# Column-tiled attention work gathered into bursts of four head groups, with a third dense PSUM bank

## Chip, cores, metric

One core of one Trainium2 chip. The metric is the time of one execution on the device in microseconds (us), median of several runs.

## The reference, cut to what matters

```python
def _A_ref(x, wq, wk, wv, wo, beta):      # S=2048, D=1024, H=32 heads of Dh=32, N=4 segments of L=512
    ...
    for s in range(N):
        logits = jnp.einsum('bhqd,bhkd->bhqk', qs, ks) * scale + mask     # causal within the segment
        a_dot = jnp.einsum('bhqk,bhkd->bhqd', _softmax(logits), vs)
        pq = phi(qs)
        num = jnp.einsum('bhld,bhde->bhle', pq, M)                        # memory of earlier segments
        den = jnp.einsum('bhld,bhd->bhl', pq, z)[..., None] + 1e-06
        outs.append(g * num / den + (1.0 - g) * a_dot)
        pk = phi(ks)
        M = M + jnp.einsum('bhld,bhle->bhde', pk, vs)
        z = z + jnp.einsum('bhld->bhd', pk)
    ...
h  = x + _A_ref(_layernorm(x), A_wq, A_wk, A_wv, A_wo, A_beta)
h2 = h + _B_ref(_layernorm(h), B_w1, B_w3, B_w2)      # (silu(h w1) * (h w3)) w2, F=3584
```

## The kernel before

The kernel first writes down all operations as a graph, then a list scheduler with a cost model of its own fixes the order of each engine, once, as the program is built. A table named SHIFT moves the priorities of single steps; it was tuned by search. Each engine is given its list in that order, with semaphores where it needs the work of another.

TensorE (PE below) works in three modes: full 128x128 matmuls (projections, output projection, feed-forward, memory), scores tiled in four blocks of 32 rows (one 32-wide head each), and probabilities times values, tiled in four blocks of 32 columns. A *mode run* is an unbroken sequence of matmuls in one mode; a *seam* is the change from one mode to the next. Four heads make a head group; there are eight in each of four segments. Scores of one operation fill PSUM banks 0 to 3, ScalarE takes their exponential in one instruction, GpSimd masks the diagonal blocks. Then one column-tiled run computes the numerator (bank 4) and the denominator (bank 5) of one head group. In the code `et` holds the exponentials, `pq` is phi of the queries, and `Mb` (or `Mbf`) and `zsel` hold the memory M and z:

```python
    def dense_group(self, late=False):                  # all full-mode work rotates through two banks
        g = Group([(6,), (7,)],
                  ("att", [(4,), (5,), (0,), (1,), (2,), (3,)]) if late else None, True)
    ...
    def pair(self, s, pr):                              # two head groups a, b: five score operations
        ta = self.scores(s, [(a, 0, 0)])
        tb = self.scores(s, [(a, 3, 384), (a, 1, 0)])
        tc = self.scores(s, [(a, 2, 0), (b, 2, 256)])
        self.finish(s, a, ...)                          # column run of a
        ta = self.scores(s, [(b, 0, 0)])
        tb = self.scores(s, [(b, 3, 384), (b, 1, 0)])
        self.finish(s, b, ...)                          # column run of b
    ...
    def finish(self, s, g, pq, pieces):
        gn, gd = self.queue(4), self.queue(5)
        ...                                             # memory read: Mb x pq to bank 4, zsel x pq to bank 5
        def emit(e, gr):
            for what, kc in order:                      # 2 x 4 key chunks x 4 heads = 32 matmuls
                b = (gn if what == "n" else gd).banks[0]
                for j in range(4):
                    r = slice(32 * j, 32 * j + 32)
                    lhsT = v[:, kc, g, r] if what == "n" else self.ones32[:, :]
                    ins.append(e.matmul(self.ps[r, b * 512 + 128 * kc:(b + 1) * 512], lhsT,
                                        pieces[kc][:, j, :], ..., tile_position=(0, 32 * j)))
        ...
        # then, per head group, on VectorE: transpose of bank 5, reciprocal, spread back by
        # transposes, and numerator x reciprocal read straight from bank 4
```

In the scheduler's model a change of mode costs PE 105 ns (`SWITCH = 105.0`).

The softmax here doesn't subtract the row's maximum and nothing guards it: scores larger than these inputs give would overflow.

Of the kernel before, what the change touches and what calls it, by code (L numbers as in the profile page):

```python
# [8 lines left out]
ALU = mybir.AluOpType  # L9
# [9 lines left out]
    0: (-342, 0), 1: (-212, 0), 2: (315, 0), 3: (-6, 1), 4: (101, 1), 5: (384, 0), 6: (-38, -1),  # L19
    7: (122, 0), 8: (556, 0), 9: (281, 0), 10: (-218, 0), 11: (-173, 1), 12: (92, 0),  # L20
    13: (-735, 1), 14: (323, 0), 15: (210, -1), 16: (-189, 0), 17: (-979, 0), 18: (265, 0),
    19: (414, 1), 20: (812, 0), 21: (7, 0), 22: (-103, -1), 23: (-657, 1), 24: (40, -1),
    25: (51, 0), 26: (-292, 0), 27: (612, 0), 28: (-340, 0), 29: (-227, 0), 30: (188, 0),
    31: (-321, -1), 32: (-2, 0), 33: (4, 0), 34: (388, 0), 35: (368, 1), 36: (-278, -1),
    37: (-458, -1), 38: (-508, 0), 39: (-303, 0), 40: (-61, 0), 41: (-280, 0), 42: (-55, 0),
    43: (-21, 0), 44: (-7, 0), 45: (4, 0), 46: (-6, -1), 47: (24, 0), 48: (38, 0), 49: (21, 0),
    50: (22, 0), 51: (134, 0), 52: (-162, -1), 53: (-133, 0), 54: (644, 0), 55: (76, -1),
    56: (-700, 1), 57: (80, 1), 58: (10, 0), 59: (-308, 0), 60: (-682, 1), 61: (-29, 0),
    62: (637, 0), 63: (-187, -1), 64: (-20, 0), 65: (11, 0), 66: (-3, 0), 67: (-210, -1),
    68: (-668, -1), 69: (2, 0), 70: (-662, 0), 71: (4, 0), 72: (11, 0), 73: (85, 0), 74: (8, 0),  # L30
    75: (9, 0), 76: (-10, 0), 77: (-18, 0), 78: (-424, 1), 79: (-9, 0), 81: (4, 0), 82: (-3, 0),
    83: (656, 0), 84: (-370, 0), 85: (2, 0), 86: (-540, 0), 87: (-294, 0), 88: (-87, 0),
    89: (-186, 0), 90: (-4, 0), 91: (39, 0), 92: (47, 0), 93: (-178, 1), 94: (68, 0),
    95: (-77, -1), 96: (138, 0), 97: (-1331, 0), 98: (-563, 1), 99: (-902, 0), 100: (421, -1),
    101: (446, 0), 102: (956, 1), 103: (87, 0), 104: (-505, -1), 105: (229, -1), 106: (573, -1),
    107: (325, 0), 108: (61, 0), 109: (312, -1), 110: (-29, -1), 111: (-643, -1), 112: (509, 1),
    113: (1416, 1), 114: (-608, -1), 115: (29, 0), 116: (283, 0), 117: (11, 0), 118: (-372, 1),
    119: (158, 1), 120: (-538, 0), 121: (-447, 0), 122: (42, 0), 123: (-489, 1), 124: (980, 0),
    125: (-266, 1), 126: (46, 1), 127: (-514, 1), 128: (-469, 1), 129: (-522, -1),
    130: (-229, 0), 131: (-210, 1), 132: (-1177, 1), 133: (270, 1), 134: (158, 0), 135: (-8, 0),  # L40
    136: (-47, 1), 137: (-1057, 0), 138: (29, 0), 139: (-110, 0), 140: (-355, -1),
    141: (-284, 0), 142: (-49, 0), 143: (-109, 0), 144: (-709, 1), 145: (40, 1), 146: (-104, 0),
    147: (-4, 0), 148: (-579, 0), 149: (-21, 0), 150: (43, 0), 151: (281, -1), 152: (131, 1),
    153: (-257, -1), 154: (-13, 0), 155: (-55, 0), 156: (20, 0), 157: (52, 0), 158: (224, -1),
    159: (-30, 0), 160: (240, -1), 161: (161, 0), 162: (-21, 0), 163: (-245, -1),
    164: (-118, 1), 165: (-21, 0), 166: (-32, 0), 167: (-330, 1), 168: (-643, -1),
    169: (373, -1), 170: (79, -1), 171: (790, -1), 172: (1, 0), 173: (117, 0), 174: (-3, 0),
    175: (-82, -1), 176: (19, -1), 177: (-1009, -1), 178: (116, 0), 179: (41, 0), 180: (63, -1),
    181: (-4, 0), 182: (-84, -1), 183: (-321, -1), 184: (-374, 0), 185: (332, 0),
    186: (-385, 0), 187: (410, 0), 188: (47, 0), 189: (83, -1), 190: (847, 0), 191: (-320, -1),  # L50
    192: (328, 0), 193: (-577, -1), 194: (-101, 0), 195: (-1451, 1), 196: (-91, 0),
    197: (583, -1), 198: (90, 0), 199: (-229, 1), 200: (-723, 1), 201: (-152, 1),
    202: (-627, 1), 203: (48, 0), 204: (280, 0), 205: (41, 0), 206: (344, 1), 207: (-444, 0),
    208: (-567, -1), 209: (-278, -1), 210: (54, 0), 211: (153, 0), 212: (-267, 0),
    213: (380, 1), 214: (-438, 1), 215: (649, 1), 216: (851, 0), 217: (954, -1), 218: (-218, 0),
    219: (130, 1), 220: (348, 0), 221: (-71, -1), 222: (-788, 0), 223: (-750, 0), 224: (-94, 0),
    225: (220, 1), 226: (6, -1), 227: (-279, 1), 228: (-660, -1), 229: (96, -1), 230: (213, 1),
    231: (270, 0), 232: (-172, 0), 233: (-91, 0), 234: (-773, 0), 235: (103, -1),
    236: (-161, 0), 237: (89, 0), 238: (-205, -1), 239: (486, -1), 240: (-177, 0),
    241: (-150, 0), 242: (-352, 0), 243: (-260, 0), 244: (44, -1), 245: (-107, 0),  # L60
    246: (174, -1), 247: (44, 0), 248: (19, 0), 249: (-252, 0), 250: (-441, 0), 251: (-26, 0),
    252: (41, 0), 253: (11, 0), 254: (30, 0), 255: (688, -1), 256: (764, 0), 257: (-364, 1),
    258: (-52, 0), 259: (17, 0), 260: (124, -1), 261: (18, 0), 262: (-206, 0), 263: (47, 0),
    264: (-179, 0), 265: (244, 0), 266: (-625, -1), 267: (93, 0), 268: (345, 0), 269: (-62, 1),
    270: (132, 0), 271: (836, 1), 272: (-541, 0), 273: (-49, -1), 274: (49, -1), 275: (-89, 1),
    276: (64, 0), 277: (-306, 1), 278: (-125, 0), 279: (-41, -1), 280: (-760, 0), 281: (213, 0),
    282: (264, -1), 283: (252, 1), 284: (-39, 0), 285: (-388, 0), 286: (-156, 1),
    287: (-713, -1), 288: (-309, -1), 289: (-975, 1), 290: (-695, 0), 291: (73, 0),
    292: (158, 0), 293: (174, 0), 294: (721, 0), 295: (166, 0), 296: (61, -1), 297: (-412, 1),
    298: (-61, -1), 299: (403, 0), 300: (59, 0), 301: (-53, 0), 302: (-52, 0), 303: (31, 0),  # L70
    304: (-297, -1), 305: (744, -1), 306: (201, -1), 307: (24, 0), 308: (-166, 0), 309: (74, 1),
    310: (327, 0), 311: (-160, 0), 312: (181, 0), 313: (-750, -1), 314: (-245, 0),
    315: (-612, 0), 316: (300, 0), 317: (-492, 0), 318: (39, 0), 319: (-48, 0), 320: (554, 0),
    321: (1, 0), 322: (-118, 0), 323: (304, -1), 324: (-636, -1), 325: (-454, -1),
    326: (-727, 0), 327: (-79, 1), 328: (-195, 1), 329: (-254, 1), 330: (678, 0),
    331: (-332, -1), 332: (164, 1), 333: (-102, 0), 334: (535, 0), 335: (-105, -1),
    336: (-708, 0), 337: (71, 0), 338: (124, 0), 339: (-288, 0), 340: (-155, 1),
    341: (-179, -1), 342: (9, 0), 343: (-423, -1), 344: (-103, 0), 345: (-407, 0), 346: (27, 1),
    347: (17, -1), 348: (-96, 0), 349: (-655, -1), 350: (-229, 1), 351: (-289, -1),
    352: (-65, 0), 353: (-196, 1), 354: (-41, 1), 355: (21, -1), 356: (582, 0), 357: (-490, 1),  # L80
    358: (843, 0), 359: (520, 0), 360: (-823, 0), 361: (-30, -1), 362: (202, 0), 363: (-203, 1),
    364: (-305, 0), 365: (-433, 0), 366: (-311, 0), 367: (-161, 0), 368: (-53, 0),
    369: (-59, 0), 370: (635, 0), 371: (12, 0), 372: (9, 0), 373: (15, 0), 374: (233, 0),
    375: (-416, -1), 376: (179, 0), 377: (-757, -1), 378: (-331, 0), 379: (-42, -1),
    380: (21, 0), 381: (-340, -1), 382: (-768, 0), 383: (102, -1), 384: (224, 0),
    385: (-181, 1), 386: (148, 0), 387: (426, 0), 388: (249, 1), 389: (133, -1), 390: (346, 0),
    391: (-513, -1), 392: (211, 0), 393: (-434, -1), 394: (134, 0), 395: (100, 0),
    396: (147, -1), 397: (-333, -1), 398: (277, -1), 399: (-32, 0), 400: (-287, 0),
    401: (-117, 0), 402: (-11, 0), 403: (92, -1), 404: (-88, 0), 405: (-239, -1), 406: (148, 0),
    407: (-639, -1), 408: (65, 1), 409: (14, -1), 410: (393, -1), 411: (-251, 0), 412: (316, 0),  # L90
    413: (-180, -1), 414: (252, 1), 415: (-47, 0), 416: (182, 0), 417: (-336, 0),
    418: (-321, 0), 419: (-879, 0), 420: (-332, -1), 421: (252, 0), 422: (-453, 1),
    423: (-5, 0), 424: (28, -1), 425: (-319, -1), 426: (-202, 0), 427: (-22, 0), 428: (333, 0),
    429: (-129, -1), 430: (139, 1), 431: (-66, -1), 432: (-200, 1), 433: (-770, 1),
# [64 lines left out]
class Graph:  # L159
# [150 lines left out]
    def schedule(self):  # L310
# [33 lines left out]
        def can_start(o):  # L344
            g = o.group
            if isinstance(g, Both):
                todo = [x for x in g.parts if x.banks is None]
                for x in todo:
                    if x.after is not None and x.after.banks is None:
                        return False  # L350
# [919 lines left out]
```

## Time and profile before

| | before |
|---|---|
| median | 910.39 us (909.82 to 911.53; the 3 runs known when the prediction was made) |
| span of the profiled run | 908.6 us |
| PE busy | 900.9 us, 99% |
| VectorE, ScalarE, GpSimd busy | 432.4, 293.0, 174.7 us |
| mode runs of PE | 95 full, 80 row-tiled, 32 column-tiled |

The prediction shows the lines of this profile on which it rests. One more piece of PE's timeline shows what a wait looks like there, as against the short extra time at a change of mode (columns: start, length, engine, line, output<-inputs, shape, count; in brackets the idle time before and what ended it):

```profile
36.08 1.02 PE L697 MATMUL ps<-xnT,wp 128*128 128x512 bf16 x4 [0.43 <-ACT kT L720]
37.76 0.40 PE L994 MATMUL ps<-qT,kT 32*128 32x128 bf16 x8 [0.66 <-ACT et L1007]
```

These are 0.43 and 0.66 us in which PE stood still for ScalarE. A change of mode leaves no bracket: it shows only as a distance between two starts that is longer than the columns need.

*Excess* is the time from one run of a mode to the next, less its columns at 2.4 columns per ns (in tiled runs four tiles stream at once, so a quarter of that), less 2.5 ns for each full matmul. It holds both mode changes and waits; a wait ahead of a run falls to the run before it.

### The profile page before, as it was taken

The numbers are of one execution on the slowest core, as the hardware profiler recorded it, in microseconds if no ns is written. First come the engines' busy times: TensorE is split into PE (matmuls) and PEld (weight loads), VectorE is DVE, ScalarE is ACT, GpSimd is POOL, SyncE is SP. The second block draws the span as 40 slices with busy tenths as digits, with TensorE's granted clock in tenths as the row PEclk, the third lists the DMA queues.
The fourth block names the chain that finished last, engine by engine and source line by source line (L and its number), as shares of the span: only waits on it lengthen the run. The fifth ranks groups of instructions, "written<-read, shape, count | busy, mean of one in ns | idle before, by whom it ended". The sixth has DMA issues, their size and how long they took to land.

```text
span 908.6 us, 13100 instructions
## 1 busy us (share of the span) xinstructions
PE 900.9 (99%) x5564; PEld 406.9 (45%) x5564; DVE 432.4 (48%) x742; ACT 293.0 (32%) x311; POOL 174.7 (19%) x273
## 2 busy tenths in 40 slices
PE   8999999999999999999999999999999999999998
PEld 5444444444444344444444444444444444444445
DVE  3777878768776764554442332211343334431111
ACT  5877776677766711111111110000121111110000
POOL 3544645565564410000000000000000000000000
PEclk9999999999999999999999999999999999999999
DMA  9976663824264164827161222012123212301110
GB/s 297 248 186 186 140 174 94 210 66 119 84 163 116 48 217 131 201 77 174 54 167 47 70 70 69 24 47 78 51 86 93 70 50 67 93 24 40 35 41 30
DMA packets 146425, 96.27 MB, mean 106 GB/s; under 512 B 45376, under 2 KB 133568, under 8 KB 146368
## 3 DMA queue, kind: packets, MB, share of 16 engines
q1 hardware_dynamic: 146368, 95.45, 38.3%
q8 instruction: 44, 0.72, 0.3%
q14 instruction: 13, 0.11, 0.0%
HBM read 76.55 MB, written 8.39 MB: 93 GB/s over the span
## 4 chain that ended last, share of the span: by engine, by line
PE 97%; DMA 1%; ACT 1%; DVE 0%; issue 0%; SPq 0%
PE ps L697 90%; PE ps L1064 4%; PE ps L994 3%; DMA wp<-in_A_wq_dram 1%; ACT et L1007 1%; DMA xs<-in_A_x_dram 0%; ACT xnT L720 0%; PE ps L709 0%; SPq L294 0%; ACT kT L720 0%; DVE xs L826 0%; DVE ob L1180 0%; DVE lnst L817 0%
## 5 line engine op out<-in xcount | busy, mean ns | idle before, releaser
L697 PE MATMUL ps<-hnT,w1b 128*128 128x512 bf16 x896 | 219.5, 379 | 0.0
L697 PE MATMUL ps<-hnT,w3b 128*128 128x512 bf16 x896 | 219.0, 379 | 0.4 <-DVE t L1151 0.3
L1148 ACT ACTIVATE sg<-ps 128x512 bf16<-128x512 f32 x112 | 66.9, 597 | 430.4 <-PE ps L697 430.3
L697 PE MATMUL ps<-w2b,hm 128*128 128x512 bf16 (+1 forms) x924 | 199.0, 373 | 0.0
L1151 DVE SCALAR_TENSOR_TENSOR t<-sg,ps 128x512 bf16<-128x512 bf16 x112 | 76.9, 687 | 209.5 <-ACT sg L1148 209.3
L1007 ACT ACTIVATE et<-ps 128x2048 bf16<-128x2048 f32 x80 | 149.9, 1874 | 40.5 <-PE ps L1064 22.5
L697 PEld LDWEIGHTS ps<-w2b,hm 128*128 128x128 bf16 x924 | 90.4, 98 | 103.3
L697 PEld LDWEIGHTS ps<-hnT,w3b 128*128 128x128 bf16 x896 | 87.0, 98 | 107.0 <-issue 2.3
L697 PEld LDWEIGHTS ps<-hnT,w1b 128*128 128x128 bf16 x896 | 87.4, 98 | 105.6 <-issue 7.9
L1012 POOL TENSOR_SCALAR_AFFINE_SELECT et<-et 128x512 bf16<-128x512 bf16 x128 | 88.6, 709 | 121.9 <-ACT et L1007 121.7
L1156 DVE SCALAR_TENSOR_TENSOR hm<-t,ps 128x512 bf16<-128x512 bf16 x112 | 76.8, 686 | 43.4 <-PE ps L697 40.8
L1180 DVE TENSOR_TENSOR ob<-hr,ps 128x512 bf16<-128x512 bf16 (+1 forms) x33 | 22.1, 671 | 125.0 <-PE ps L697 125.0
L697 PE MATMUL ps<-xnT,wp 128*128 128x512 bf16 (+1 forms) x352 | 62.0, 321 | 1.9 <-ACT xnT L720 1.5
L697 PE MATMUL ps<-hnT,wp 128*128 128x512 bf16 x256 | 62.5, 380 | 0.3 <-DMA wp<-in_A_wq_dram 0.3
L697 PE MATMUL ps<-wo,oT 128*128 128x512 bf16 x256 | 62.5, 379 | 0.0
L697 PEld LDWEIGHTS ps<-xnT,wp 128*128 128x128 bf16 x352 | 27.7, 98 | 28.7 <-issue 4.2
L1075 DVE STREAM_TRANSPOSE T<-ps 128x512 f32<-128x512 f32 x32 | 22.9, 716 | 31.4 <-PE ps L1064 31.3
L697 PEld LDWEIGHTS ps<-wo,oT 128*128 128x128 bf16 x256 | 24.1, 98 | 29.7 <-issue 2.1
L697 PEld LDWEIGHTS ps<-hnT,wp 128*128 128x128 bf16 x256 | 23.3, 98 | 30.3 <-issue 3.8
L1101 POOL TENSOR_TENSOR Nm<-Nm,R1b 128x512 f32<-128x512 f32 x23 | 29.2, 1271 | 23.6 <-DVE R1b L1090 23.6
L994 PE MATMUL ps<-qT,kT 32*128 32x128 bf16 (+3 forms) x512 | 31.7, 301 | 0.8 <-ACT et L1007 0.8
L823 POOL TENSOR_SCALAR lnve<-lnmv 128x1 f32<-128x1 f32 x31 | 8.3, 268 | 125.0 <-DVE lnmv L819 125.0
(84 smaller groups left out, 614.2 us busy)
## 6 DMA issues: line engine op xcount, KB each, us to landing
w1b<-in_B_w_dram SPq DMA_DIRECT2D x28, 512.0 KB, 3.9
w3b<-in_B_w_dram SPq DMA_DIRECT2D x28, 512.0 KB, 3.8
wp<-in_A_wv_dram SPq DMA_DIRECT2D x8, 1024.0 KB, 6.8
wp<-in_A_wq_dram SPq DMA_DIRECT2D x7, 1024.0 KB, 5.6
wp<-in_A_wk_dram SPq DMA_DIRECT2D x7, 1024.0 KB, 6.4
w2b<-in_B_w_dram SPq DMA_DIRECT2D x7, 1024.0 KB, 8.0
xs<-in_A_x_dram SPq DMA_DIRECT2D x16, 256.0 KB, 5.5
h<-in_A_x_dram SPq DMA_DIRECT2D x16, 256.0 KB, 3.7
```

Of the source, the lines that this page charges most:

```text
L697: return [e.matmul(p[0](gr), p[1], p[2], start=p[3], stop=p[4]) for p in part]
L823: self.pool_op(lambda e: e.tensor_scalar(ve, var, self.EPS, None, op0=ALU.add), 1, [var], [ve], 0)
L994: ins.append(e.matmul(self.bank(gr, j, 512 - 128 * kc, off), k[r, g, 128 * kc:128 * kc + 128], q[r, g, 128 * kc:512], start=True, stop=Tru ...
L1007: return [e.activation(et[:, :, :], src, AF.Exp, scale=self.scale)]
L1012: self.pool_op(lambda e, m=m: e.affine_select(m, m, pattern=[[0, 4], [1, 128]], compare_op=ALU.is_ge, fill=0.0, base=0, channel_multiplier ...
L1064: ins.append(e.matmul(self.ps[r, b * 512 + 128 * kc:(b + 1) * 512], lhsT, pieces[kc][:, j, :], start=kc == 0 and (what == "n" or s == 0), ...
L1075: G.op("dve", dve_ns(512), lambda e, gr: [e.transpose(T1, self.bank(gr))], writes=[T1], cls=0, group=gd)
L1101: self.either(lambda e: e.tensor_tensor(Nm, Nm, R1, op=ALU.mult), 512, 2, [Nm, R1], [Nm], 2)
L1148: self.g.op("act", act_ns(512), lambda e, gr, sg=sg: [e.activation(sg, self.bank(gr), AF.Tanh, scale=0.5)], writes=[sg], cls=2, group=gg)
L1151: e.scalar_tensor_tensor(t1, sg, 1.0, self.bank(gr), op0=ALU.add, op1=ALU.mult)], reads=[sg], writes=[t1], cls=2,
L1156: e.scalar_tensor_tensor(dst, t1, 0.5, self.bank(gr), op0=ALU.mult, op1=ALU.mult)], reads=[t1], writes=[dst], cls=2,
L1180: self.g.op("dve", dve_ns(n), lambda e, gr, hs=hs, ob=ob, n=n: [e.tensor_tensor(ob, hs, self.bank(gr, 0, n), op=ALU.add)], reads=[hs], wri ...
```

## The change

The intent is fewer changes of mode: ten score operations of four head groups come first, then one burst of column work for all four, with all denominators in one operation and one bank. That needs ten probability buffers and copies of the numerators out of PSUM; it frees bank 5 for dense work, and the numerator's memory read now goes through the dense banks too. The diff, cut to its core (the table SHIFT, retuned for the new graph, fills over a third of the original and is left out):

```diff
     def dense_group(self, late=False):
-        g = Group([(6,), (7,)],
-                  ("att", [(4,), (5,), (0,), (1,), (2,), (3,)]) if late else None, True)
+        g = Group([(5,), (6,), (7,)],
+                  ("att", [(4,), (0,), (1,), (2,), (3,)]) if late else None, True)
...
-    def attention(self, s):
-        for pr in range(4):
-            ...
-            self.pair(s, pr)
+    def attention(self, s, half):
+        for i, parts in enumerate((
+                [(a, 0, 0)], [(a, 3, 0), (a, 1, 128)], [(a, 2, 0), (b, 2, 256)],
+                [(b, 0, 0)], [(b, 3, 0), (b, 1, 128)],
+                [(c, 0, 0)], [(c, 3, 0), (c, 1, 128)], [(c, 2, 0), (d, 2, 256)],
+                [(d, 0, 0)], [(d, 3, 0), (d, 1, 128)])):
+            self.scores(s, g0, i, parts, at)
+            if s == 0 and half == 1 and i in (3, 5, 7, 9):
+                self.g.dma(self.wo[...], ...)          # wo in four pieces; before: one load at the start
+        self.finish(s, g0, at)
...
+        column(gd, range(4), lambda i, kc, j: self.ones32[:, i, :], ...)      # 64 matmuls, bank 4
+        for n, i in enumerate((3, 0, 1, 2)):
+            gn[i] = self.queue(n)                                             # banks 0 to 3
+            column(gn[i], [i], lambda i, kc, j: v[:, kc, g0 + i, 32 * j:32 * j + 32], ...)
...
+        # one transpose T1 of bank 4 and one reciprocal for four groups; per group a copy Nsb of the
+        # numerator out of PSUM by ScalarE or VectorE, one spread of double width, then from SBUF
```

Also in the change: one buffer each for pq, Mbf, zsel and pkn (before: two), two h buffers for three, a third projection-weight buffer that shares memory with an output buffer, phi without its separate relu pass, and in the first segment v after q and k.

## The prediction

> **What bounds the kernel now.** I read the page from its head: busy times, slices, chain of work; then the waits of the tensor engine (PE), then its timeline in order.
>
> ```profile
> span 908.6 us, 13100 instructions
> PE 900.9 (99%) x5564; PEld 406.9 (45%) x5564; DVE 432.4 (48%) x742; ACT 293.0 (32%) x311; POOL 174.7 (19%) x273
> ...
> PE   8999999999999999999999999999999999999998
> ...
> PE 97%; DMA 1%; ACT 1%; DVE 0%; issue 0%; SPq 0%
> ```
>
> PE is busy in every slice, and 97% of the chain that ended last is PE. No other engine reaches half. So a microsecond counts only if PE gives it up. The chain by pieces, cut to the end of the span, shows how the time divides:
>
> ```profile
> 326.89 1.20 PE ps L1064 x32
> 328.09 577.87 PE ps L697 x2704
> ```
>
> The last 578 us are one unbroken run of 2704 matmuls of the dense feed-forward layer, which the change does not touch. Attention and its projections lie before 328 us. The waits of PE as a whole:
>
> ```profile
> PE ps L697 <- ACT xnT L720: 1.5, 2, 1.2
> PE ps L697 <- DVE oT L751: 1.2, 1, 1.2
> PE ps L994 <- ACT et L1007: 0.8, 2, 0.7
> PE ps L697 <- ACT kT L720: 0.4, 1, 0.4
> PE ps L697 <- DVE t L1151: 0.3, 1, 0.3
> PE ps L697 <- DMA wp<-in_A_wq_dram: 0.3, 1, 0.3
> ```
>
> They sum to 5 us; 2.98 us of that (first two rows and a 0.2 us row) fall before 13 us, while x loads and is normalized. Only 2.1 us of true waiting is left in the attention part. So PE is bound by its own instruction stream, and the question is what in that stream is not useful streaming. The timeline of PE shows it:
>
> ```profile
> 144.48 0.40 PE L994 MATMUL ps<-qT,kT 32*128 32x128 bf16 x8
> 144.81 1.04 PE L697 MATMUL ps<-wo,oT 128*128 128x512 bf16 x4
> 145.77 0.73 PE L1064 MATMUL ps<-et,v 128*32 128x512 bf16 x16
> 146.33 0.72 PE L1064 MATMUL ps<-et,ones 128*32 128x128 bf16 x16
> 146.97 1.90 PE L697 MATMUL ps<-hnT,wp 128*128 128x512 bf16 x8
> 148.71 0.38 PE L697 MATMUL ps<-pq,zsel 128*128 128x512 bf16 x1
> ...
> 167.40 0.40 PE L994 MATMUL ps<-qT,kT 32*128 32x128 bf16 x8
> 167.72 0.73 PE L1064 MATMUL ps<-et,v 128*32 128x512 bf16 x16
> 168.28 0.72 PE L1064 MATMUL ps<-et,ones 128*32 128x128 bf16 x16
> 168.93 1.04 PE L697 MATMUL ps<-hnT,wp 128*128 128x512 bf16 x4
> ```
>
> Columns: start, length (pipelined, so only starts may be subtracted), line, shape, count. Three modes alternate: full 128*128, row-tiled scores 32*128 (L994), column-tiled 128*32 (L1064). Eight full matmuls take 148.71-146.97 = 1.74 us, 0.217 each. Four before a column run take 145.77-144.81 = 0.96, where 4 x 0.216 = 0.86: **0.10 us extra** at the seam. The column run takes 146.97-145.77 = 1.20 us; at 2.4 columns a nanosecond its two passes of 512+384+256+128 columns, four tiles at once, are 2 x 1280/2400 = 1.07: **0.13 us extra**. A row run takes 144.81-144.48 = 0.33 against 512/2400 = 0.21: **0.12 us extra**. All start times sorted this way give, outside waits, 0.137 us for each column run, 0.113 to 0.12 for a row run, and 0.11 for each full run entered from another mode, plus 2.5 ns for each full matmul. From 1.24 us to the last matmul PE takes 904.5 us against 863.6 of pure streaming: 40.9 of overhead, of which some 24 is mode changes.
>
> **What the Trainium skill says.** "TensorEngine Tiling (Array Packing)", Key Properties: "Mode switching requires drain: Changing tiling mode (not just tile) drains the TensorE". It gives no time; this trace gives 0.11 to 0.14 us each. "TensorE: Matmul & The Clock Gate", section "Wait — 56ns, not 53.3ns?": a warm matmul costs N/2.4 ns plus about 2.5. The trace agrees: the last run is 2648 x 512 and 56 x 256 columns, 570.9 us, plus 2704 x 0.0025 = 6.8, together 577.7 against 577.87 measured. "Perfetto Trace Analysis", Optimizing Tensor Performance, Matmuls: independent groups should rotate through different PSUM banks so that evacuation overlaps. That is the purpose of the third dense bank, but with 2.1 us of waiting in all, this trace offers it little.
>
> **The change, part by part.**
>
> Column runs. Today there is one per head group and segment, 4 x 8 = 32, each holding numerator and denominator. In the trace 17 of them directly follow a row run, one directly precedes one, 14 stand between dense runs. The change makes one burst per four groups, so 8: a denominator operation of 64 matmuls, then four numerator operations of 16. Instruction count and columns streamed are the same (8 x 8 x 0.533 = 34.1 us before and after). Saved entries: 24 x 0.137 = 3.3 us.
>
> Full runs. The trace has 95 today: 80 row runs and 32 column runs, 18 of them abutting. After it, 80 row runs stay, as every score operation still fills the same four banks and must wait for a 1.87 us exponential before the next. The 8 bursts are mostly isolated, since the last masks of a burst take a microsecond or so after the last exponential, in which dense work runs. So about 88 full runs: (95-88) x 0.11 = 0.8 us. This is why the saving is not 24 x 0.25 = 6: more than half of today's column runs already share a seam with scores.
>
> The memory read (Mbf, zsel) keeps 24 + 24 full matmuls; the transposes, projections and memory update keep their counts. Warm-up stays.
>
> Vector, scalar and GpSimd. Per four groups the change removes three of four 0.716 us transposes of denominators and three of four 0.32 us reciprocals (the one left is four times as long, at most 1.3 us by the same row), replaces two 0.7 us spreads by one of double width, and drops a relu pass. It adds copies out of PSUM (32 instead of 24 of about 0.69 us) and GpSimd multiplications of 1.27 us. With DVE, ACT and POOL at 7 or 8, 6 or 7 and 5 or 6 tenths in the attention part, all of this lies beside PE: 0 us on the path.
>
> The third dense bank (5, 6, 7 for 6, 7), evacuation ahead of other work, wo loaded later and first-segment v after q and k act on waits alone. At most 2.1 us; I give them half, 1.0 us.
>
> Sum: 3.3 + 0.8 + 1.0 = 5.1 us off 910.4, so **905.3 us**.
>
> **Rivals.** (1) *The burst starves PE.* Ten scores must finish before the columns: 10 x 1.87 = 18.7 us of exponentials, about 1 of masks, 4.4 of columns, 0.7 of evacuation, so 25 us per burst and 8 x 25 = 200 us in series. The attention part has some 300 us, and a segment holds 41 us of next projections, 14 of output projection and 19 of attention on PE, 74 against 50. For the last segment there are 24 feed-forward tiles of 16 matmuls writing into space that the third segment left free, 82 us. So there is enough to fill with. Against: buffers get tighter (one pq, one Mbf, two weight buffers late, two h buffers), while weight loads of 1 MB take 5.6 to 6.8 us to land. Today one such load costs 0.3 us. If some of these bite, add 2 to 6 us: 907 to 911.
> (2) *The start gains more.* At 35 to 38 us PE waits 1.1 us and some row and full runs stretch by another 0.5; with wo (2 MB, 11.1 us to landing) out of the way while DMA is 99% and 88% busy in the first 40 us, and q and k first, first-segment scores flow sooner. That could take 1 to 2 us more: 903.
> (3) *The seams cost differently.* If the five column operations do not run together (numerators need no denominator, so dense work may slip between while masks are pending), 8 more runs cost 8 x 0.25 = 2 us: 907. If bursts abut score runs, 1 us is gained.
> (4) *Another engine becomes the bound.* Nothing speaks for it: DVE's highest slice is 8 tenths, its work falls.
>
> **Range and chances.** The central sum is small and rests on counts; the error is in waits. The good ends of 2 and 3 give 902, the bad ends of 1 and 3 give 909 to 911. I take 901.5 to 908.5 as holding it 8 times in 10. Faster by 2% needs 18 us, three quarters of all mode changes now paid, while 80 row runs stay: 3%. Slower by 2% would need 18 us of new waits in a schedule whose order was fixed anew for the change: 2%. Within 2%: 95%.
>
> **What would show it.** Right: about 8 column runs of some 4.4 us in PE's timeline, about 80 row runs, 88 full runs, an unbroken tail of about 2700 matmuls in 578 us, PE at 99%, waits of PE outside the start under 2 us. Each step wrong: column runs in 16 or more pieces (step one); a column burst much longer than 4.4 us, so that a seam is hidden inside it; PE waits on ACT or DVE near bursts or on weight loads (rival 1); first dense work much earlier than 13 us (rival 2). A time under 900 would mean that row seams went too, or that PE dropped instructions that I counted as kept.

## The result

| | before | after |
|---|---|---|
| median | 910.96 us (909.82 to 911.77, 4 runs) | 905.65 us (904.67 to 906.68, 4 runs) |
| ratio after / before | | 0.9943, 95% interval 0.9926 to 0.9960 |
| span of the profiled run | 908.6 us | 905.0 us; 903.8 us in a second profile |

Ratios here are the mean time of one kernel's fast runs over that of the other's of the same rounds, so not quite the ratio of the medians. The change gained 0.6%: clear of the noise, but "the same" at a threshold of 2%.

The head of the profile page after. The first pair is the first profile, in which 88 matmul records are missing (5476 of 5564); the second pair is that of the same kernel in experiment 1, with all records:

```profile
span 905.0 us, 12909 instructions
...
PE 890.9 (98%) x5476; PEld 409.4 (45%) x5564; DVE 420.5 (46%) x643; ACT 285.2 (32%) x299; POOL 179.9 (20%) x248
```

```profile
span 903.8 us, 12997 instructions
...
PE 897.1 (99%) x5564; PEld 409.4 (45%) x5564; DVE 420.1 (46%) x643; ACT 285.2 (32%) x299; POOL 180.3 (20%) x248
```

The row of the first profile would read as if PE had 10 us less work than before. It had not: the number of weight loads, 5564, is the same in both, and the matmuls that lack a record turn up as 17 "issue" waits of 0.2 us. For this reason all accounts below use the second profile. A burst in its timeline of PE:

```profile
50.79 2.36 PE L1054 MATMUL ps<-et,v 128*32 128x512 bf16 x64
52.97 2.35 PE L1054 MATMUL ps<-et,ones 128*32 128x512 bf16 x64
55.25 2.76 PE L706 MATMUL ps<-wp,xnT 128*128 128x512 bf16 x12
57.95 0.39 PE L1009 MATMUL ps<-qT,kT 32*128 32x512 bf16 x4
```

The 128 column matmuls take 55.25-50.79 = 4.46 us where their columns need 8 x 1280/2400 = 4.27: 0.19 us extra for a burst, where four separate runs before cost 4 x 0.137. Nothing dense slips in between, and dense work follows before the next scores. Part of the cost of a column run grows with its length: by start times the mean excess is 0.127 us for runs of 16 matmuls and 0.156 for runs of 64 (both in experiment 4), 0.137 for runs of 32 (before) and 0.197 for the bursts of 128. All four fit an entry of 0.116 us and 0.63 ns for each matmul. Merging runs saves only the entry. The chain that ended last, its two longest pieces at the end:

```profile
317.14 4.46 PE ps L1054 x128
321.60 579.64 PE ps L706 x2712
```

So the unbroken tail stays what it was (before: 577.87 us for 2704 matmuls; eight more of 0.216 us each are now in it), and the gain lies before it. What PE waits for after:

```profile
PE ps L706 <- DVE oT L761: 1.2, 1, 1.2
PE ps L718 <- DVE xs L817: 1.0, 1, 1.0
PE ps L706 <- DMA w3b<-in_B_w_dram: 0.7, 1, 0.7
PE ps L706 <- DMA pkn<-pk: 0.5, 1, 0.5
```

The first two belong to the start, before 9 us. Of the waits on ScalarE at 36 to 38 us, 0.2 us is left. Two are new: at 302 us for a weight load that landed late, and at 212 us for the transposing load of pkn. That load was issued at 207.66 us, just as the last matmul that read the single pkn buffer ended (207.59), though its source had been ready at 201.1. The account of the whole stream:

| part of the PE stream | before: runs, excess us | after: runs, excess us | difference |
|---|---|---|---|
| start, up to the first scores | 1, 4.42 | 1, 4.06 | -0.36 |
| row-tiled runs | 80, 9.89 | 80, 10.84 | +0.95 |
| full runs between | 93, 12.05 | 87, 9.50 | -2.55 |
| column-tiled runs | 32, 4.37 | 8, 1.58 | -2.79 |
| tail | 1, 0.11 | 1, 0.16 | +0.05 |
| pure streaming, and 2.5 ns per full matmul | 863.61 + 10.07 | 863.61 + 10.07 | 0 |
| sum (first matmul to the end of the last) | 904.53 | 899.81 | -4.72 |

The spans differ by 908.6-903.8 = 4.8 us, the medians by 5.3. Of the 4.72 us, entries are 24 x 0.116 = 2.79 for column runs and 6 x 0.108 = 0.65 for full runs, so 3.4; the other 1.3 us is waits, as net of what went and what came.

### The profile page after: what moved, and what is told of

It reads as the page before. It is cut to its first block, busy times and chain, and to the rows that moved or that the text cites. A ratio compares the mean times of both kernels' runs of the same rounds, so it can differ in the third digit from the quotient of the medians.

```text
span 905.0 us, 12909 instructions
## 1 busy us (share of the span) xinstructions
PE 890.9 (98%) x5476; PEld 409.4 (45%) x5564; DVE 420.5 (46%) x643; ACT 285.2 (32%) x299; POOL 179.9 (20%) x248
## 4 chain that ended last, share of the span: by engine, by line
PE 96%; DMA 2%; issue 1%; DVE 1%; ACT 0%; SPq 0%; POOL 0%; ACTq 0%
PE ps L706 89%; PE ps L1054 4%; PE ps L1009 3%; DMA wp<-in_A_wv_dram 1%; DMA xs<-in_A_x_dram 1%; DMA pkn<-pk 1%; ACT et L1021 0%; DVE hm L1179 0%; DVE t L1174 0%; SPq L297 0%; PE ps L718 0%; DVE oT L1125 0%; DVE R L1122 0%; DVE lnst L827 0%; ACT sg L1171 0%
## 5 line engine op out<-in xcount | busy, mean ns | idle before, releaser
L706 PE MATMUL ps<-hnT,w3b 128*128 128x512 bf16 x882 | 216.7, 379 | 2.2 <-DVE hm L1179 1.5
L706 PE MATMUL ps<-w2b,hm 128*128 128x512 bf16 (+1 forms) x905 | 196.5, 372 | 1.0
L1030 POOL TENSOR_SCALAR_AFFINE_SELECT et<-et 128x512 bf16<-128x512 bf16 (+1 forms) x96 | 82.1, 862 | 93.0 <-ACT et L1021 93.0
L706 PE MATMUL ps<-hnT,wp 128*128 128x512 bf16 x248 | 59.7, 380 | 0.9 <-issue 0.6
L706 PE MATMUL ps<-xnT,wp 128*128 128x512 bf16 (+1 forms) x344 | 59.6, 320 | 0.9 <-issue 0.6
L1108 DVE STREAM_TRANSPOSE R<-Rc 128x1024 f32<-128x1024 f32 (+1 forms) x32 | 35.0, 1099 | 0.3
L706 PE MATMUL ps<-wp,xnT 128*128 128x512 bf16 x122 | 30.3, 380 | 0.7 <-issue 0.6
```

Source lines behind the costliest of these rows:

```text
L706: return [e.matmul(p[0](gr), p[1], p[2], start=p[3], stop=p[4]) for p in part]
L1030: self.pool_op(lambda e, v=v, pat=pat: e.affine_select(v, v, pattern=pat, compare_op=ALU.is_ge, fill=0.0, base=0, channel_multiplier=-1), ...
L1108: sp = self.dve_op(lambda e, dst=dst, src=src: e.transpose(dst, src), dve_ns(512 * nr), [Rc[:, i, 0:nr, :]], [rs], 1)
```

## The experiments

The theory: a run pays about 0.11 to 0.14 us whenever PE enters it from another mode, so the gain is the number of runs saved, plus some 1 us of waits. Rivals: it came from the third dense bank or the other buffers; from the retuned order; from the wo load, out of the way of the start; or from VectorE's smaller load. Every kernel here gave a correct result. Each was timed in five rounds.

### 1. The kernel after, again (after_again)

No edit.

> The changed kernel once more, to firm up its gain. Seam theory (fewer changes of tiling mode on the tensor engine, 24 column runs and 6 full runs fewer, 3.3 + 0.65 us, plus under 1 us of waits): 4 to 5.5 us below the kernel before, ratio 0.994 to 0.9955. The one new wait of 1.5 us near 302 us, behind VectorE, should be there again if it is the order of the instructions and not chance; if it was chance, it is gone and the span is near 903.5.

Measured: 905.63 us (904.67 to 906.12), ratio to before 0.9938 (0.9926 to 0.9951). The record of PE is complete this time. The first profile had, at the same place:

```profile
303.39 0.55 PEld L706 LDWEIGHTS ps<-hnT,w3b 128*128 128x128 bf16 x4 [1.58 <-DMA w3b<-in_B_w_dram]
303.62 0.81 PE L706 MATMUL ps<-hnT,w3b 128*128 128x512 bf16 x3 [1.51 <-DVE hm L1179]
```

There the matmul's wait was 1.51 us and was put down to VectorE; in this run it is 0.74 us and put down to the weight load. The trace of the first profile settles it: there too the load of w3b came last. It landed at 303.35 us, and PE's own loading of the weights (PEld, the first row) began at 303.39. Four loadings but only three matmuls stand there: the record of the first matmul is missing, so the wait looks 0.2 us too long and its end is put down to something else. So the wait is the same one in both, longer or shorter as w3b lands at 303.35 or at 302.23. "Behind VectorE", in the expectation, was an artefact of the missing record.

### 2. Dense work between abutting scores and columns in the kernel before (before_isolated)

In the finished order of the kernel before, for 16 of the 17 column runs that directly follow scores, the next ready dense operation (four matmuls, in one place eight) is moved between; full runs go from 95 to 110:

```diff
+            if o.mode == "col" and out and out[-1].mode == "row":
+                for d in pe[i:i + 60]:          # next full-mode operation whose inputs are done
+                    ...
+                        out.append(d)
+            out.append(o)
```

> The kernel before with a dense operation moved between each column run and the row run ahead of it: 32 column runs as before, but 1 instead of 17 abuts a row run in front; 110 full runs instead of 95. Seam theory, with each entry into a full run priced at 0.108 us: 15 x 0.108 = +1.6 us, ratio 1.0015 to 1.002. Rival (a column run costs its 0.25 us wherever it stands, so that the prediction's discount for abutting runs was wrong): 0.

Measured: 915.54 us, ratio 1.0050 (1.0037 to 1.0063): +4.6 us. The expectation was missed in size. In the account, full runs gained 15.58-12.05 = 3.5 us of excess, of which 15 x 0.108 = 1.6 is entries; the rest is waits, because scores and columns were held up by 0.86 us of dense work (four matmuls) each. In the tail stands one gap of 1.1 us, 612 matmuls in, for which the wait view names nothing (experiment 5 has its cause). The edit was too coarse to weigh a seam.

### 3. Dense work between the column operations after (split_columns)

The same kind of edit in the kernel after, with the denominator operation cut in four: 62 column runs and 123 full runs.

```diff
-        column(gd, range(4), lambda i, kc, j: self.ones32[:, i, :], ...)
+        for a in range(4):
+            column(gd, [a], lambda i, kc, j: self.ones32[:, i, :], ...)
+            if o.mode == "col" and out and out[-1].mode == "col":
+                ...                             # next ready full-mode operation goes between
```

> The changed kernel with its column bursts cut into pieces by moving dense matmuls in between: 62 column runs instead of 8, 122 full runs instead of 89, the same matmuls, banks, buffers and third dense bank. Seam theory: 62 x 0.137 - 8 x 0.205 = +6.9 us, 33 x 0.108 = +3.6 us, two row runs fewer -0.2, so some +10 us over the changed kernel (about 916, above the kernel before). Rival (the gain is the third dense bank, the single reciprocal or the new order): within 2 us of the changed kernel, about 906 to 908.

Measured: 946.46 us, ratio 1.0388 (1.0374 to 1.0403): +41 us over the kernel after, four times what was expected. The waits of PE, 26 us in all where the kernel after has 4, say why it is no test of the seam; the two largest are:

```profile
PE ps L1033 <- ACT et L1045: 5.8, 6, 2.0
PE ps L1033 <- DVE Nsb L1125: 3.3, 3, 1.2
```

L1033 is the scores. With the burst stretched, everything behind it comes late: the next scores wait for exponentials and for the copies out of banks 0 to 3. An order that was fixed for one set of durations is fragile against coarse moves.

### 4. Single matmuls in the gaps of a burst (split_gently)

In each burst, four matmuls that one ready dense operation has anyway are issued one at a time in the four gaps between column operations. Nothing is added, no operation changes its place by more than a burst: 40 column runs, 121 full, 80 row-tiled.

```diff
+            part = d.emit.__defaults__[0]       # d: a ready dense operation of four matmuls
+            for k in range(3):
+                ahead(cols[k + 1], d, part[k:k + 1])
+            ...                                 # the fourth before the last column operation
+            out += cols[:4] + [d, cols[4]]
```

> The cut bursts again, without holding them up: in each of the 8 bursts the four matmuls of one dense operation that follows it, whose inputs were ready long before, are put singly into the four gaps between the five column operations. 40 column runs instead of 8, 121 full runs instead of 89, the same 80 row runs, each burst 1.9 us longer. Seam theory: 40 x 0.137 - 8 x 0.197 = +3.9 us, 32 x 0.108 = +3.5 us, so +7.4 us over the changed kernel: about 913, ratio 1.002 to the kernel before. In its records the mean excess of a column run should be 0.137 and of an entry into a full run 0.108. Rival (seams are hidden by something; the 41 us of the crude cut were all waits): within 2 us of the changed kernel.

Measured: 914.32 us (913.99 to 915.08), ratio to before 1.0037 (1.0024 to 1.0049), so +8.7 us over the 905.63 of after (+8.4 over the kernel of experiment 7, which ran on the same chip and is as fast as after). Its timeline of PE, one cut burst:

```profile
51.00 0.73 PE L1107 MATMUL ps<-et,v 128*32 128x512 bf16 x16
51.66 0.39 PE L759 MATMUL ps<-wp,xnT 128*128 128x512 bf16 x1
51.98 0.73 PE L1107 MATMUL ps<-et,v 128*32 128x512 bf16 x16
52.64 0.39 PE L759 MATMUL ps<-wp,xnT 128*128 128x512 bf16 x1
52.96 0.73 PE L1107 MATMUL ps<-et,v 128*32 128x512 bf16 x16
```

A column operation takes 51.66-51.00 = 0.66 us (columns alone 0.533), a single dense matmul 51.98-51.66 = 0.32 (0.216 in a row of its own kind). No bracket: nobody is waited for. The account over the kernel after: column runs +3.72 us for 32 more, 0.116 each; full runs +5.21, of which 32 x 0.107 = 3.4 is entries and some 1.8 waits. The times lie above those of the kernel before, with the same buffers, banks and engine loads as after. This carries the theory: the same matmuls in more mode runs lose what the change gained.

### 5. Single matmuls between scores and columns before (isolate_gently)

The mirror of it: one matmul of a ready dense operation goes between scores and columns in 14 of the 17 places in the kernel before; the count of column runs stays, full runs go from 95 to 109.

```diff
+            if o.mode == "col" and i and pe[i - 1].mode == "row":
+                ...                             # d: ready dense operation further on
+                            whole(e, d.group, part[:1])     # its first matmul, then the column run
```

> The kernel before with one single dense matmul, ready long before, moved between a column run and the row run ahead of it, at 14 of the 17 places where they abut: 109 full runs instead of 95, all else as it was. Seam theory: 14 x 0.108 = +1.5 us, ratio 1.0015. If a column run costs the same wherever it stands: 0.

Measured: 913.47 us (912.28 to 913.88), ratio 1.0023 (1.0010 to 1.0035): +2.4 us. In the account, full runs have 13.56-12.05 = 1.51 us more, and 14 x 0.108 = 1.51. Column runs stay at 4.36. So a column run that follows scores pays the same as one that follows dense work, and what an isolated place costs more is the re-entry into full mode. The rest is row-tiled runs (+0.5) and one stall in the tail, 1.2 us (the account adds up to +3.2 and not +2.4, as the profiled run of the kernel before was one of its fast ones):

```profile
330.04 132.20 PE ps L721 x612
462.24 1.17 issue
```

The chain of experiment 2 has the same stall after the same 612 matmuls. The views put it down to "issue", but the traces show its cause: the matmul behind it is the first that reads w2, and the last of the seven loads of w2 landed at 463.31 us here, the weight load of PE that needs it starting at 463.37 (in experiment 2: 465.31 and 465.37). From issue to landing that load took 8.8 us in both edited kernels and 7.3 in the kernel before, where it landed at 459.92, 0.09 us ahead of its first use at 460.01. So the order of the kernel before has no slack there; why the load took longer is not shown. In the kernel after it lands 134 us ahead of its first use.

### 6. More work on VectorE inside the burst (more_dve)

Three passes of statistics over the denominators' bank are put ahead of its transpose, in each of the eight bursts (a result that nothing uses):

```diff
         G.op("dve", dve_ns(512), lambda e, gr: [
+            e.bn_stats(self.junk[:, n + i, :], self.bank(gr)) for i in range(3)] + [
             e.transpose(T1, self.bank(gr))], ...)
```

> The changed kernel with three more VectorE passes over the denominators' bank in each burst (24 x 0.69 = 16.5 us of VectorE time, as much as the three transposes that the change removed, at the same place). If VectorE lies beside the tensor engine, as predicted: 0 to 1 us more. If the full VectorE after the bursts of the last segment is a second bound: the wait near 302 us grows by up to 2 us, in sum +2 to +4. If the shared reciprocal chain is on the path and is where the gain came from: +8 to +16.

Measured: 914.49 us (914.39 to 914.97), ratio to before 1.0037 (1.0024 to 1.0049): +8.9 us over after for 8 x 1.9 = 15 us of VectorE work, though VectorE is busy only 48% of the time. PE's waits:

```profile
PE ps L1010 <- DVE Nsb L1103: 4.9, 4, 1.3
...
PE ps L707 <- DVE T L1079: 0.8, 1, 0.8
```

VectorE's timeline after one burst, with the extra passes, and then without:

```profile
94.16 1.89 DVE L1078 BATCH_NORM_STATS2 junk<-ps 128x6 f32<-128x512 f32 x3 [0.36 <-PE ps L1055]
95.97 0.70 DVE L1079 STREAM_TRANSPOSE T<-ps 128x512 f32<-128x512 f32 x1
96.59 0.71 DVE L1103 TENSOR_SCALAR Nsb<-ps,ocol 128x512 f32<-128x512 f32 x1
```

```profile
92.82 0.72 DVE L1075 STREAM_TRANSPOSE T<-ps 128x512 f32<-128x512 f32 x1 [0.36 <-PE ps L1054]
93.46 0.71 DVE L1099 TENSOR_SCALAR Nsb<-ps,ocol 128x512 f32<-128x512 f32 x1
```

VectorE starts 0.36 us after the burst in both, and each thing behind the transpose is 1.8 us later. The next scores need banks 0 to 3, so they wait for the copy (Nsb); the next memory read needs bank 4, so it waits for the transpose. Over half of the delay comes through, some 1.1 us of 1.9 per burst: by this, VectorE has a slack of rather under 1 us right behind a burst. The result lies in the range that was set for the rival, that the gain came from VectorE's shorter chain. But it shows what longer work there costs, not what shorter work gained: in the kernel before, PE waited for VectorE only 0.5 us after the start (the rows for t and R0b, 0.3 and 0.2), so a shorter chain can hardly have removed more than that.

### 7. wo early again (wo_early)

In the kernel after, the four pieces of wo are issued at 14 us and not from 71 us on; nothing else moves.

```diff
+        k = next(i for i, o in enumerate(sp) if o.start > 14500.0)
+        order["sp"] = sp = sp[:k] + moved + sp[k:]
```

> The changed kernel, its order on every engine kept, with the four loads of wo put back to where the kernel before has its one load, ahead of the second half of the first weights. If the later wo helped the start (rival 2 of the prediction): waits of the tensor engine on weight loads between 20 and 60 us, +1 to +4 us. If the transfer is hidden anyway: 0, at most 0.5.

Measured: 905.90 us (905.38 to 906.05), ratio to before 0.9943 (0.9929 to 0.9956): no change against after. The load is really there, in the queue's timeline:

```profile
13.93 1.96 SPq L298 DMA_DIRECT2D wo<-in_A_wo_dram  x4
```

and it lands more slowly (9.8 us median for a piece, 7.0 in the kernel after), but the excess of the start is 4.19 us against 4.06. In the kernel after it is hidden either way.

### 8. Two dense banks after (two_banks_ordered)

Dense work gets banks 6 and 7 only while attention runs, as before; bank 5 serves the memory read alone. The fixed order was made for three banks, so SHIFT was searched anew with the kernel's own scheduler.

```diff
-        g = Group([(5,), (6,), (7,)],
-                  ("att", [(4,), (0,), (1,), (2,), (3,)]) if late else None, True)
+        g = Group([(6,), (7,)],
+                  ("att", [(5,), (4,), (0,), (1,), (2,), (3,)]) if late else None, True)
...
-            gm = self.dense_group()
+            gm = Group([(5,)], None, True)
...
                 gg, gu = self.dense_group(True), self.dense_group(True)
+                gu.after = (gg,)
```

> The kernel after with its dense work kept to two PSUM banks (the third is used by the memory read alone), and its order of operations searched anew for that. It keeps 8 column runs, 80 row runs and 89 full runs. The theory of changes of mode says that the entries are what was saved, so the time stays within 2 us of the kernel after: about 906 to 907.5 us, some 4 us below the kernel before. The rival, that the third dense bank is what gained the time, says that it goes back to about 910 us.

Measured: 904.06 us (904.02 to 904.30), ratio to before 0.9926 (0.9913 to 0.9938). This is below what was expected, below the kernel after and the fastest of all. So the gain does not need the third dense bank. Its runs are 8, 80 and 89 like those of after, its full and column excess is 9.68 and 1.57 us (after: 9.50 and 1.58); what is lower is that of the row-tiled runs, 9.22 us against 10.84. Its profile lists four waits of PE, of which the first three lie before 10 us:

```profile
PE ps L713 <- DVE oT L768: 1.2, 1, 1.2
PE ps L725 <- DVE xs L824: 1.1, 1, 1.1
PE ps L725 <- DVE xs L843: 0.8, 1, 0.8
PE ps L713 <- DVE t L1182: 0.2, 1, 0.2
```

So this order leaves PE practically no wait in the attention part. 9.22 us over 80 runs is 0.115 each: bare changes of mode.

### 9. The kernel before with its order searched anew (before_ordered)

Only SHIFT differs. 32 column, 80 row-tiled, 91 full runs.

> The kernel before, nothing changed but the table that sets its order, searched anew; 32 column runs, 80 row runs and 91 full runs instead of 95. The rival, that the new order in the change is the gain, says that it comes near 906 us. The theory of changes of mode says 4 full entries of 0.11 us, so -0.4 us, and up to 1.2 us of waits that a better order may fill: 909.3 to 910.5 us.

Measured: 910.15 us (909.62 to 911.15), ratio 0.9993 (0.9980 to 1.0005). Full runs lost 1.8 us of excess, but a wait of 0.9 us now stands inside the column runs' account and waits of 1.2 us stand in the tail: 0.76 us at 421.8 us, behind a late operation of VectorE, and 0.44 at 460.2 us for the same load of w2 as in experiment 5 (landed at 460.14, needed from 460.20). Even without these it would be near 909. This new order alone does not give the gain.

### 10. The kernel after with its order searched anew (after_ordered)

Only SHIFT differs.

> The kernel after, nothing changed but the table that sets its order, searched anew; the same 8, 80 and 89 runs. The count of changes of mode is the same, so only waits can go: -0.5 us, 905 us, between 904 and 906 us. This is the candidate for a version better than both.

Measured: 905.89 us (905.69 to 906.87), ratio to before 0.9944 (0.9931 to 0.9958). The expectation of 0.5 us less was missed; PE still waits 0.89 us for the load of w3b, at 303 us. This was meant as the better version; experiment 8 is it, 1.8 us below this one on the same chip. What part of that is the partition of banks and what the luck of the search, these runs do not separate.

## Why the prediction was right, and where it was off

The time was predicted as 905.3 us, in 901.5 to 908.5, and measured as 905.65; the mechanism holds too, by experiments 4 and 5. That the sum came so near is in part luck: 0.5 us too much for the column runs and 0.3 too little for the waits all but cancel. By the steps of the sum:

- **Column runs, 3.3 us.** Measured 2.79. The count was right, 8 isolated bursts with nothing in them (the numerators went first, not the denominators as the step said). The price was not: the 0.137 us of a run are an entry of 0.116 and 32 x 0.63 ns = 0.02 that its matmuls cost wherever they stand. Only the entries were saved: 24 x 0.116 = 2.79.
- **Full runs, 0.8 us.** 89 runs and not 88, so 6 x 0.108 = 0.65 us. That abutting runs already shared a seam, which is why the step did not claim 6 us for both, is what experiment 5 measured: 0.108 us for each place pulled apart.
- **Waits, half of 2.1 us.** The size came near by two larger terms of opposite sign. Of the 2.55 us that full runs lost, 2.55-0.65 = 1.9 is waits that are gone; the start gave 0.36; and 0.95 us came back in row-tiled runs. Net 1.3. Nearly all of the 0.95 is itself net of waits: 0.80 us for the load of w3b at 302 us, 0.55 for pkn at 212 and 0.23 at 186 came, 0.67 that the kernel before had at 35 and 316 us went. So 2.6 us of old waits went in the attention part (1.9 and 0.67), more than the 2.1 that the step had as the most: that was read from the wait view, which shows less than the start times. The step gave the third dense bank a part in it; experiment 8 shows a kernel without it that waits even less. Which of the other alterations took the old waits away is not shown.
- **80 row runs stay, work unchanged.** Right: 80, 5564 matmuls, 863.61 us of streaming in both.
- **VectorE, ScalarE and GpSimd lie beside PE, 0 us.** True for the work as it is, VectorE's falls from 432 to 420 us. But "7 or 8 tenths busy" was no reason for it. Experiment 6 shows that of 1.9 us of extra VectorE work at the wrong place, right behind a burst, about 1.1 reach PE.

Of the rivals: (1) *the burst starves PE* did not come true as told; the one bite of tighter buffers that the trace shows is the pkn wait at 212 us, 0.5 us, as pkn has one buffer now. The late weight load at 302 us (0.74 us, about 1.3 in the first profile) is no clear case: w1 and w3 have two buffers each in both kernels. (2) *The start gains more* fell: the first scores came later (19.39 us, before 17.57), and by experiment 7 the wo load does not matter in the kernel after. (3) *The seams cost differently* fell: the bursts run whole. (4) fell with the profile.

Open: why the last load of w2 took 8.8 us and not 7.3 in experiments 2 and 5, and what delays the load of w3b at 302 us.

## What to carry to other kernels

When one engine is busy all the time, account for its stream to the last tenth of a microsecond by start times: work, a constant per instruction, and so many changes of mode; then a regrouping is worth the number of runs it really takes away, and runs of two tiled modes that already abut save less. Compare runs of different lengths before pricing a run: what grows with its matmuls is not saved by merging. Fine edits to a fixed order (a single matmul moved) measure such a price; coarse ones measure the fragility of the order. An engine that is half idle can still be critical for a microsecond at a time, where it frees a buffer that the bound engine wants next.

## What the Trainium skill lacked or had wrong

- "TensorEngine Tiling (Array Packing)", Key Properties, says that a change of mode drains TensorE and gives no time. Here an entry into full mode costs 0.106 to 0.108 us, a row-tiled run 0.115 where nothing else waits, a column-tiled run 0.116 and 0.63 ns more for each of its matmuls; whether scores or dense work came before made no difference (4.37 and 4.36 us for the 32 column runs of experiment 5's two kernels).
- "TensorE: Matmul & The Clock Gate", Back-to-back issue gap, gives about 131 ns as the sustained spacing of matmuls of N=512 in a real kernel and says that N/2.4+2.5 counts too much. In this real stream of loads and matmuls the formula holds: 2712 matmuls (56 of them 256 wide) in 579.64 us, 0.2137 us each, where the formula gives 579.4 in all.
- The same page, LDWEIGHTS (loading the stationary operand), makes a load proportional to its columns, P/1.2 ns. For 128 and 32 columns that would be 107 and 27 ns (an estimate from the page's formula). By the length of its records the kernel after takes 98 and 97 ns (line, engine, operation, tiles, shape, count, busy us, mean ns):

```profile
L706 PEld LDWEIGHTS ps<-wo,oT 128*128 128x128 bf16 x256 | 24.0, 98 | 29.3 <-issue 2.4 <-DMA h<-in_A_x_dram 0.3
...
L1054 PEld LDWEIGHTS ps<-et,ones 128*32 128x32 bf16 x512 | 12.1, 97 | 5.3
```

- The pages on reading a profile, "Perfetto Trace Analysis" and "NEFF Inspection", don't say that it can lack matmul records: 88 of 5564 in one, which read as 17 waits for "issue" (2.7 us in all) and as 6 us less of PE work, and in one place made a wait look 0.2 us longer and put it down to the wrong engine.
